# A transformer block with dilated local attention and an MLP gate: order of the layer norms, runs of the softmax sums, and the queues of two kinds of DMA

## The chip, the cores and the metric

The kernel runs on one core of one Trainium2 chip. The metric is the device time of one execution in microseconds (us). The core has a matrix engine (PE, with its weight loads shown apart as PEld), a vector engine (DVE), a scalar engine (ACT), GpSimd (POOL), and a queue processor (SP) that only issues DMAs. Every engine works through its own instructions strictly in the order in which they stand in its queue; instructions of different engines wait for each other by semaphores.

## The reference

The input is x of 2048 rows and 512 columns in bf16. What is computed, cut to what matters:

```python
def _A_ref(x, wqkv, wo):                  # 32 heads of 16, window W = 8, dilation dil = 2
    q, k, v = ...                         # x @ wqkv, split by heads
    idx = pos[:, None] - off[None, :]     # off = arange(8) * 2: rows i, i-2, ..., i-14
    logits = einsum("bhsd,bhswd->bhsw", q, kg) * Dh ** -0.5
    logits = where(mask, logits, -1e9)
    return (softmax(logits) @ vg).reshape(B, S, D) @ wo

def _B_ref(x, w1, w2, w3, w4):            # F = 1376
    h = gelu(layernorm(x) @ w1)
    hs = concat([rows -1, +1, -2, +2 of the four column groups of h]) @ w2
    x1 = x + hs
    return x1 + gelu(layernorm(x1) @ w3) @ w4

xn = layernorm(x)
out = x + _A_ref(xn) * silu(_B_ref(xn))
```

Since the dilation is 2, a row attends only to rows of its own parity. The kernel therefore splits the 2048 rows into two parities of 1024 rows (index p), in which the window is 8 neighbouring rows.

## The kernel before, in words

**Chunks.** The 1024 rows of each parity are two chunks of 512 rows, so there are four chunks c = 0 to 3 with p = c // 2. Each chunk passes through these stages:

- `stage_a(c)` (L184): the layer norm of the chunk (`layer_stats`, L173: statistics on DVE, the inverse root on POOL; the normalisation L197 on DVE), 16 transposes on PE into `tr_ps` (L203) and their copy to `xnT` (L205), a row of scales from the second layer norm (`r2`, L189 to L216), then the products for q and k (L224), and w1 with a gelu (L240, L244) into `hT`. Four stages write `hT`.
- `stage_b(c)` (L260): the product with w2 over shifted rows of `hT` (L268), the residual add on DVE (L273), a layer norm (`l3` tiles), a store of the normalised chunk to DRAM (`x1n_dram`, L281) and its transposed load as `x1nT` (L285). `stage_b(0)` needs `hT` of chunks 0 and 2; `stage_b(1)` needs chunk 3 as well.
- `stage_w3(c)` (L291): 44 products of w3 with `x1nT` (L301), each pair followed by a gelu (L306) into `h3T`.
- `w4_tile(c, jj)` (L310): one tile of 128 rows: 11 products with w4 (L317), one with the identity that adds x1 (L321), and the gate (L323 on ACT, L324 on DVE). There are 16 of them.

The tiles of the statistics of both layer norms, `st`, `mv` and `rstd`, share their tags, with two buffers each, in the pool `small`.

**Attention units.** Each parity is nine units of up to 120 query rows (the first has 128, the last 56). `scores(p, u)` (L333) makes v (L339, copied by DVE at L343), the logits `s_ps` (L359), four exponentials on ACT (L366) and two masks on DVE (L369). `weighted(p, u, ...)` (L375) makes the 32 small products `o_ps` (L387), of which each 32-row group holds 16 rows of outputs and the sums of the softmax, and copies them to two `orw` tiles, one on ACT (L396) and one on DVE (L398).

**Runs and normalisation.** The nine units of a parity form two runs: units 0 to 4 (608 rows) and units 5 to 8 (416 rows). After the last unit of a run, `normalise(p, r)` (L402) issues, all on SP's queue:

- two stores of the sums to DRAM (L410) and one load of them, spread over 128 partitions, as `dn` (L413);
- eight DMAs that repack the outputs from `orw` to `oT` (L417), 16 partitions each;
- after the reciprocal on DVE (L423), a store of it (L424) and four broadcast loads as `rr` (L427).

It ends with a DVE product of `oT` with `rr` (L431). The two `orw` tiles of a run and its `rr` take their buffers from one pool, `sm5`, with three buffers.

**The end.** `final_tile(p, i)` (L435) loads one tile of 128 rows of x as `xt` (L437, two buffers), multiplies `oT` with wo (L440, four products), multiplies with the gate (L445) and adds x (L446) on DVE into `sg` (two buffers), and stores it (L447). Load and store are on SP's queue.

**Order.** The program text gives the order of priority; at build time the framework lists the instructions of each engine in that order as its own model of the durations finds them ready and their buffers free, so an instruction can stand ahead of an earlier one that is not ready in the model. On the chip each engine keeps the list. The main body reads (L450 to L480):

```python
    for c in range(3):
        stage_a(c)
    stage_b(0); stage_a(3); stage_b(1); stage_w3(0); stage_b(2)
    stage_w3(1); stage_b(3); stage_w3(2); stage_w3(3)
    for n, (p, u) in enumerate(order):        # 18 units
        cur = (p, u) + scores(p, u)
        if fill: fill.pop(0)()                # one w4_tile for each unit
        if prev is not None: weighted(*prev)
        if n >= 13: final_tile(0, n - 13)
```

followed by the rest of the final tiles: three of the first parity and eight of the second.

## Time and profile before

| what | value |
|---|---|
| median of the two timed runs | 289.62 us (288.32 and 290.92) |
| profiled execution, its own time | 291.65 us |
| its span, first to last instruction | 289.9 us |
| mean granted clock of PE in it | 0.926 of full speed |
| busy in the span | PE 225.9, DVE 154.5, ACT 136.7, POOL 18.5 us |
| DMA moved | 21.31 MB, 73 GB/s on average |

The profile is of one execution. Its views used below are: the page with the busy time of each engine and the chain of work that ended last; a table by stage, where each row is a stretch of the span with the busy time of each engine, the granted clock (1.00 is full speed) and the busy share of the 16 DMA engines; the list of waits (who waited for whom: total us, times, longest); and the timeline. In it, PE's busy time is that of pipelined matmuls, whose single durations overlap.

### The profile page before, as it was taken

The numbers are of one execution on the slowest core, as the hardware profiler recorded it, in microseconds if no ns is written. First come the engines' busy times: TensorE is split into PE (matmuls) and PEld (weight loads), VectorE is DVE, ScalarE is ACT, GpSimd is POOL, SyncE is SP. The second block draws the span as 40 slices with busy tenths as digits, with TensorE's granted clock in tenths as the row PEclk, the third lists the DMA queues.
The fourth block names the chain that finished last, engine by engine and source line by source line (L and its number), as shares of the span: only waits on it lengthen the run. The fifth ranks groups of instructions, "written<-read, shape, count | busy, mean of one in ns | idle before, by whom it ended". The sixth has DMA issues, their size and how long they took to land.

```text
span 289.9 us, 4239 instructions
## 1 busy us (share of the span) xinstructions
PE 225.9 (78%) x1704; PEld 98.7 (34%) x1704; DVE 154.5 (53%) x273; ACT 136.7 (47%) x164; POOL 18.5 (6%) x42
## 2 busy tenths in 40 slices
PE   0599999508999899949899999889979997491470
PEld 0344444204444344414233434333334333130120
DVE  5676240666053717200276667586677777562453
ACT  1065848100836262505977777748877666200000
POOL 2344000041001010000000000000000000000000
PEclk9999999965999999989979999999999999957588
DMA  6997000025002323230000002410310126314443
GB/s 186 352 376 234 3 0 0 0 72 75 0 0 75 72 76 69 75 72 1 0 2 0 2 1 42 91 59 6 66 62 0 38 45 136 119 37 110 130 145 109
DMA packets 28387, 21.31 MB, mean 73 GB/s; under 512 B 10992, under 2 KB 27856, under 8 KB 28368
## 3 DMA queue, kind: packets, MB, share of 16 engines
q1 hardware_dynamic: 28368, 21.04, 27.2%
q8 instruction: 13, 0.21, 0.3%
q14 instruction: 6, 0.05, 0.1%
HBM read 12.39 MB, written 4.46 MB: 58 GB/s over the span
## 4 chain that ended last, share of the span: by engine, by line
PE 44%; DMA 16%; DVE 13%; SPq 11%; ACT 9%; issue 3%; POOL 2%; POOLq 0%; DVEq 0%; ACTq 0%
PE qk_ps L224 11%; PE w_ps L317 9%; PE w_ps L301 7%; SPq L417 5%; ACT prob L366 5%; PE w_ps L240 5%; DMA xt<-in_A_x_dram 4%; DMA x1nT<-x1n_dram 3%; DMA xn_85<-in_A_x_dram 3%; PE s_ps L359 3%; DVE l3s L177 3%; PE v_ps L339 2%; SPq L427 2%; PE o_ps L387 2%; DMA rr<-rden_d_2327 2%
## 5 line engine op out<-in xcount | busy, mean ns | idle before, releaser
L366 ACT ACTIVATE prob<-s_ps 128x960 bf16<-128x960 f32 (+2 forms) x72 | 61.6, 934 | 22.4 <-PE s_ps L359 19.9
L369 DVE TENSOR_TENSOR prob<-prob,mask_126 128x1920 bf16<-128x1920 bf16 (+1 forms) x32 | 34.6, 1089 | 21.6 <-ACT prob L366 21.6
L317 PE MATMUL w_ps<-w_sb,h3T 128*128 128x512 bf16 (+1 forms) x176 | 45.0, 388 | 0.4 <-DVE v_aug_131 L343 0.3
L301 PE MATMUL w_ps<-x1nT,w_sb 128*128 128x512 bf16 (+1 forms) x176 | 40.3, 391 | 5.1 <-DMA x1nT<-x1n_dram 5.1
L306 ACT ACTIVATE h3T<-w_ps 128x1024 bf16<-128x1024 f32 x20 | 20.5, 1024 | 34.8 <-PE w_ps L301 20.9
L301 PEld LDWEIGHTS <-w_sb 128*128 128x128 bf16 (+1 forms) x176 | 17.8, 102 | 27.4 <-DMA x1nT<-x1n_dram 6.3
L317 PEld LDWEIGHTS <-h3T 128*128 128x128 bf16 (+1 forms) x176 | 15.6, 99 | 21.6 <-issue 7.6
L224 PEld LDWEIGHTS <-wqk_sb 128*128 128x128 bf16 x128 | 13.7, 108 | 18.9 <-issue 6.0
L440 PE MATMUL wo_ps<-wo_sb,oT_2325 128*128 128x512 bf16 x32 | 10.3, 474 | 12.2 <-DVE sg L445 12.2
L230 ACT ACTIVATE qm_138<-qk_ps,hmask 128x1024 bf16<-128x1024 f32 x8 | 8.4, 1113 | 22.8 <-PE qk_ps L224 22.6
L224 PE MATMUL qk_ps<-xnT_133,wqk_sb 128*128 128x512 bf16 x64 | 17.0, 427 | 1.5 <-DVE xnT_133 L205 1.5
L224 PE MATMUL qk_ps<-xnT_134,wqk_sb 128*128 128x512 bf16 x64 | 16.7, 421 | 0.6 <-DVE xnT_134 L205 0.6
L230 ACT ACTIVATE qm_137<-qk_ps,hmask 128x1024 bf16<-128x1024 f32 x8 | 8.4, 1113 | 18.1 <-PE qk_ps L224 18.1
L369 DVE TENSOR_TENSOR prob<-prob,mask_123 128x2048 bf16<-128x2048 bf16 x4 | 4.9, 1224 | 21.9 <-ACT prob L366 21.9
L273 DVE TENSOR_TENSOR xn_85<-w_ps,xn_85 128x1024 bf16<-128x1024 f32 x4 | 4.9, 1215 | 21.6 <-PE w_ps L268 21.6
L440 PE MATMUL wo_ps<-wo_sb,oT_1498 128*128 128x512 bf16 x32 | 11.7, 473 | 3.7 <-DVE v_aug_131 L343 3.7
L240 PE MATMUL w_ps<-xn2T,w_sb 128*128 128x512 bf16 x64 | 14.5, 379 | 0.0
L359 PE MATMUL s_ps<-qm_137,kT_135 32*128 32x240 bf16 (+2 forms) x144 | 11.4, 266 | 3.9 <-ACT prob L366 2.5
L398 DVE CAST orw<-o_ps 128x480 bf16<-128x480 f32 (+2 forms) x18 | 11.3, 628 | 5.0 <-PE o_ps L387 4.9
L359 PE MATMUL s_ps<-qm_138,kT_136 32*128 32x240 bf16 (+2 forms) x144 | 10.1, 259 | 5.0 <-ACT prob L366 3.4
L323 ACT ACTIVATE sig<-w_ps 128x512 bf16<-128x512 f32 x16 | 9.6, 599 | 8.1 <-PE w_ps L321 8.1
L396 ACT ACTIVATE orw<-o_ps 128x480 bf16<-128x480 f32 (+2 forms) x18 | 9.5, 551 | 6.2 <-PE o_ps L387 6.2
(104 smaller groups left out, 270.1 us busy)
## 6 DMA issues: line engine op xcount, KB each, us to landing
xt<-in_A_x_dram SPq DMA_DIRECT2D x16, 128.0 KB
out_dram<-sg SPq DMA_DIRECT2D x16, 128.0 KB
w_sb<-in_B_w_dram SPq DMA_DIRECT2D x1, 1376.0 KB
w_sb<-in_B_w_dram SPq DMA_DIRECT2D x1, 1280.0 KB
xn_85<-in_A_x_dram SPq DMA_DIRECT2D x4, 256.0 KB
wqk_sb<-in_A_wqkv_dram SPq DMA_DIRECT2D x2, 512.0 KB
w_sb<-in_B_w_dram SPq DMA_DIRECT2D x2, 512.0 KB
xn_86<-in_A_x_dram SPq DMA_DIRECT2D x4, 256.0 KB
```

The costliest lines, as they stand in the source:

```text
L224: nc.tensor.matmul(pt[:, b, :], lhsT=wqk_sb[:, dt, nt * P : (nt + 1) * P], rhs=xnT[p][:, dt, cs], start=(dt == 0), stop=(dt == ND - 1),)
L230: nc.scalar.activation(qm[p][:, 2 * a : 2 * a + 2, e, cs], pt, AF.Copy, scale=hmask[:, e : e + 1])
L240: nc.tensor.matmul(pt[:, b, :], lhsT=w1_sb[:, dt, g * P : (g + 1) * P], rhs=xn2T[:, dt, :], start=(dt == 0), stop=(dt == ND - 1),)
L301: nc.tensor.matmul(pt[:fs, ft % 2, :], lhsT=w3_sb[:, dt, ft * P : ft * P + fs], rhs=x1nT[:, dt, :], start=(dt == 0), stop=(dt == ND - 1),)
L306: last["gelu"] = nc.scalar.activation(h3T[:, 2 * a : 2 * a + 2, :], pt, AF.Gelu_apprx_tanh)
L317: nc.tensor.matmul(pt, lhsT=h3T[:fs, ft, jj * P : (jj + 1) * P], rhs=w4_sb[:fs, ft, :], start=(ft == 0), stop=False,)
L359: nc.tensor.matmul(st[:nk, b, dl * 2 * nq : (dl + 1) * 2 * nq].rearrange("k (e q) -> k e q", e=2), lhsT=kT[p][r : r + 32, dt, k0 : k0 + nk ...
L366: nc.scalar.activation(prv[:nk, jj], st[:nk, :, 0 : 4 * nq], AF.Exp, scale=SCALE)
L369: nc.vector.tensor_tensor(out=ph[:nk], in0=ph[:nk], in1=msk[:nk, 0:nq].unsqueeze(1).to_broadcast([nk, 16, nq]), op=ALU.mult,)
L398: nc.vector.tensor_copy(out=dst, in_=src)
L417: nc.sync.dma_start(out=oT[p][DH * hh : DH * (hh + 1), :, ra : ra + rw], in_=orw[p][jj][32 * cg : 32 * cg + DH, :, 0:rw],)
L440: nc.tensor.matmul(pt, lhsT=oT[p][:, dt, i * P : (i + 1) * P], rhs=wo_sb[:, dt, :], start=(dt == 0), stop=(dt == ND - 1),)
```

## The change

1. **Layer norms.** The statistics and the normalisation of `stage_a` move to a new function `stage_ln(c)`; the tiles of `l1` and `l3` get tags of their own. `stage_ln(3)` is emitted ahead of `stage_a(2)`.
2. **Order of w2 and w3.** `stage_b(2)` is emitted before `stage_w3(0)`, and `stage_b(3)` before `stage_w3(1)`.
3. **Runs.** The second parity gets three runs: units 0 to 4 (608 rows), 5 and 6 (240 rows), 7 and 8 (176 rows). The product with `rr` becomes `normalise_end`, emitted later: for the run (0, 0) at unit index 9, for (0, 1) at 13, for (1, 0) at 17, and for (1, 1) and (1, 2) among the last final tiles.
4. **Queues.** The repack DMAs (L417) are issued by POOL instead of SP. The loads of x for the end become two DMAs of 1 MB (`load_xo`, SP's queue), and the stores become eight DMAs of two tiles each on ACT's queue.
5. **Fill.** Of the w4 tiles 13 are filled in at unit indices 0 to 12 and three come after the last unit; all final tiles come after that.
6. **Buffers.** The pool `sm5` (`orw`, `rr`) goes from three buffers to four, `sm4` (weights w1 and w2, `xn2T`, `xn3`, `x1nT`, `prob`) from six to five.

```diff
-    for a, b in ((0, (NU + 1) // 2), ((NU + 1) // 2, NU)):
-        runs.append((a, b, units[a][0], sum(units[u][1] for u in range(a, b))))
-    RW = max(r[3] for r in runs)
+    for cuts in ((0, 5, NU), (0, 5, 7, NU)):
+        runs.append(
+            [(a, b, units[a][0], sum(units[u][1] for u in range(a, b))) for a, b in zip(cuts[:-1], cuts[1:])]
+        )
+    RW = max(r[3] for rs in runs for r in rs)
...
-    sm5 = ctx.enter_context(tc.tile_pool(name="sm5", bufs=3))
-    sm4 = ctx.enter_context(tc.tile_pool(name="sm4", bufs=6))
+    sm5 = ctx.enter_context(tc.tile_pool(name="sm5", bufs=4))
+    sm4 = ctx.enter_context(tc.tile_pool(name="sm4", bufs=5))
...
-        st = small.tile([P, TPC, nc.vector.BN_STATS_DIM], F32, name=name + "s", tag="st")
-        mv = small.tile([P, TPC, nc.vector.BN_AGGR_DIM], F32, name=name + "m", tag="mv")
+        st = small.tile([P, TPC, nc.vector.BN_STATS_DIM], F32, name=name + "s", tag=name + "s")
+        mv = small.tile([P, TPC, nc.vector.BN_AGGR_DIM], F32, name=name + "m", tag=name + "m")
...
-    def stage_a(c):
+    r2s = {}
+
+    def stage_ln(c):
         p, k = c // 2, c % 2
         x_c = xn[p][:, k * TPC : (k + 1) * TPC, :]
...
         rsqrt_eps(r2, r2)
+        for j in range(TPC):
+            nc.vector.tensor_scalar(
+                out=x_c[:, j, :], in0=x_c[:, j, :], scalar1=mv[:, j, 0:1], scalar2=rstd[:, j : j + 1],
+                op0=ALU.subtract, op1=ALU.mult,
+            )
+        r2s[c] = r2
...
-                nc.sync.dma_start(
+                nc.gpsimd.dma_start(
                     out=oT[p][DH * hh : DH * (hh + 1), :, ra : ra + rw],
                     in_=orw[p][jj][32 * cg : 32 * cg + DH, :, 0:rw],
                 )
...
+    def normalise_end(p, r):
+        _, _, ra, rw = runs[p][r]
         nc.vector.tensor_tensor(
-            out=oT[p][:, :, ra : ra + rw], in0=oT[p][:, :, ra : ra + rw], in1=rr[:, :, 0:rw], op=ALU.mult
+            out=oT[p][:, :, ra : ra + rw], in0=oT[p][:, :, ra : ra + rw], in1=rrs[p, r][:, :, 0:rw], op=ALU.mult
         )
 
+    def load_xo(p):
+        xo[p] = midt([P, M // P, D], f"xo{p}")
+        nc.sync.dma_start(out=xo[p], in_=xv[p].rearrange("(i q) d -> q i d", q=P))
+
     def final_tile(p, i):
-        xt = fin.tile([P, D], BF16, name="xt", tag="xt")
-        nc.sync.dma_start(out=xt, in_=xv[p, i * P : (i + 1) * P, :])
...
-        nc.vector.tensor_tensor(out=sg, in0=sg, in1=xt, op=ALU.add)
-        nc.sync.dma_start(out=ov[p, i * P : (i + 1) * P, :], in_=sg)
-
-    for c in range(3):
-        stage_a(c)
+        nc.vector.tensor_tensor(out=xo[p][:, i, :], in0=sg, in1=xo[p][:, i, :], op=ALU.add)
+        if i % 2 == 1:
+            nc.scalar.dma_start(
+                out=ov[p, (i - 1) * P : (i + 1) * P, :].rearrange("(i q) d -> q i d", q=P),
+                in_=xo[p][:, i - 1 : i + 1, :],
+            )
+
+    stage_ln(0)
+    stage_a(0)
+    stage_ln(1)
+    stage_ln(2)
+    stage_a(1)
+    stage_ln(3)
+    stage_a(2)
     stage_b(0)
     stage_a(3)
     stage_b(1)
+    stage_b(2)
     stage_w3(0)
-    stage_b(2)
+    stage_b(3)
     stage_w3(1)
-    stage_b(3)
     stage_w3(2)
     stage_w3(3)
...
+    fill = {n: [w4s[n]] for n in range(13)}
+    fill[5].append(lambda: load_xo(0))
+    fill[9].append(lambda: load_xo(1))
+    fill[9].append(lambda: normalise_end(0, 0))
+    fill[13] = [lambda: normalise_end(0, 1)]
+    fill[17] = [lambda: normalise_end(1, 0)]
...
-        if n >= 13:
-            final_tile(0, n - 13)
     weighted(*prev)
-    for f in fill:
+    for f in w4s[13:]:
         f()
-    for i in range(len(order) - 13, M // P):
+    for i in range(M // P):
         final_tile(0, i)
-    for i in range(M // P):
+    normalise_end(1, 1)
+    for i in range(6):
+        final_tile(1, i)
+    normalise_end(1, 2)
+    for i in range(6, M // P):
         final_tile(1, i)
```

More of the change, by code (lines that the diff above doesn't have):

```diff
@@ L192, in stage_a @@
         rsqrt_eps(r2, r2)
+        for j in range(TPC):
[4 more added lines that the diff above has]
+        r2s[c] = r2
+    def stage_a(c):
+        p, k = c // 2, c % 2
+        x_c = xn[p][:, k * TPC : (k + 1) * TPC, :]
+        cs = slice(k * CH, (k + 1) * CH)
+        r2 = r2s.pop(c)
         for h in range(TPC // 2):
@@ L376, in weighted @@
         q0, nq, k0, nk = units[u]
-        r = 0 if u < runs[0][1] else 1
-        ra = runs[r][2]
-        if u == runs[r][0]:
+        r = next(i for i, x in enumerate(runs[p]) if u < x[1])
+        ra = runs[p][r][2]
+        if u == runs[p][r][0]:
             orw[p] = [sm5.tile([P, ND, RW], BF16, name="orw", tag="s5") for jj in range(2)]
@@ L398, in weighted @@
                 nc.vector.tensor_copy(out=dst, in_=src)
-        if u == runs[r][1] - 1:
+        if u == runs[p][r][1] - 1:
             normalise(p, r)
+    rrs = {}
     def normalise(p, r):
-        _, _, ra, rw = runs[r]
+        _, _, ra, rw = runs[p][r]
         if r == 0:
@@ L466 @@
         cur = (p, u) + scores(p, u)
-        if fill:
-            fill.pop(0)()
+        for f in fill.get(n, ()):
+            f()
         if prev is not None:
```

13 lines of the change are left out of this document (5 added, 8 removed).

## The prediction

> **What bounds the kernel now.** I read the page first: the busy shares, then the chain that ended last.
>
> ```profile
> PE 225.9 (78%) x1704; PEld 98.7 (34%) x1704; DVE 154.5 (53%) x273; ACT 136.7 (47%) x164; POOL 18.5 (6%) x42
> PE 44%; DMA 16%; DVE 13%; SPq 11%; ACT 9%; issue 3%; POOL 2%; POOLq 0%; DVEq 0%; ACTq 0%
> ```
>
> PE is busiest, yet holds only 44% of the chain; DMA and SP's queue hold 27%. So I cut the span into stages and looked for stretches in which PE rests.
>
> ```profile
> 26.20:38.68 12.48, 11.81 (x69) 5.86 (x68) 4.21 (x10) 8.13 (x8) 1.03 (x1) 1.00 0.06 21
> 54.77:65.16 10.39, 0.01 (x2) 0.01 (x1) 8.02 (x23) 0.00 (x0) 2.88 (x6) 0.73 0.15 50
> 65.16:81.17 16.01, 15.07 (x69) 7.31 (x70) 4.77 (x11) 7.21 (x7) 1.32 (x3) 0.75 0.27 34
> 81.17:84.62 3.45, 3.45 (x17) 1.57 (x16) 1.49 (x2) 1.03 (x1) 0.00 (x0) 1.00 0.00 0
> 84.62:94.12 9.50, 9.50 (x46) 4.38 (x45) 5.07 (x13) 4.77 (x5) 1.27 (x2) 1.00 0.17 57
> 121.00:123.35 2.35, 2.32 (x11) 0.88 (x9) 0.69 (x1) 0.84 (x2) 0.00 (x0) 1.00 0.04 13
> 123.35:127.57 4.22, 0.00 (x1) 0.01 (x1) 0.00 (x0) 0.00 (x0) 0.00 (x0) 1.00 0.65 124
> 127.57:138.86 11.29, 11.29 (x45) 4.75 (x46) 0.00 (x0) 4.86 (x5) 0.00 (x0) 0.85 0.00 1
> 145.00:220.30 75.30, 68.25 (x768) 28.55 (x765) 53.18 (x65) 54.14 (x73) 0.00 (x0) 0.98 0.15 32
> 220.30:257.40 37.10, 28.82 (x341) 12.40 (x341) 25.39 (x36) 20.77 (x29) 0.00 (x0) 0.95 0.29 67
> 257.40:289.90 32.50, 13.68 (x40) 4.67 (x40) 13.55 (x26) 0.00 (x0) 0.00 (x0) 0.71 0.42 118
> ```
>
> Columns: stretch, length, busy PE, PEld, DVE, ACT, POOL, granted clock, DMA share, GB/s. The first row is an undisturbed `stage_a` (chunk 1): 12.48 us. PE then rests 10.39 us before that of chunk 3, which takes 16.01 us at a clock of 0.75. It rests 4.22 us before the last `stage_w3`, which takes 11.29 us where the first took 9.50. From 257.40 on PE is busy 13.68 of 32.50 us. The waits name the causes:
>
> ```profile
> PE tr_ps L203 <- DVE xn_86 L197: 10.4, 1, 10.4
> PE w_ps L301 <- DMA x1nT<-x1n_dram: 5.1, 2, 4.2
> PE wo_ps L440 <- DVE sg L445: 12.2, 3, 6.2
> DVE sg L445 <- DMA out_dram<-sg: 9.6, 5, 4.0
> PE wo_ps L440 <- DVE v_aug_131 L343: 3.7, 1, 3.7
> 53.09 1.24 DVE xn_85 L273
> 58.16 0.58 DVE l1s L177
> 63.62 1.05 POOL l1r L171
> ```
>
> The last three rows are of the chain: DVE does chunk 3's statistics only at 58, behind `stage_b(0)`'s add at 53.09, although x was there long before; the shared tags with two buffers explain it.
>
> **The change part by part: the front.** LN(3) is emitted ahead of `stage_a(2)`, with own tags. Its DVE and POOL work lands where DVE is busy 4.21 of 12.48 us; that PE-bound stage hides it. Chunk 3 then starts at 54.77 and is done 12.48 us later instead of 10.39 + 16.01 = 26.40: 13.9 gone. What is late next is DVE, which still owes `stage_b(0)` its work when the transposes are done:
>
> ```profile
> L273 DVE TENSOR_TENSOR xn_85<-w_ps,xn_85 128x1024 bf16<-128x1024 f32 x4 | 4.9, 1215 | 21.6 <-PE w_ps L268 21.6
> L177 DVE BATCH_NORM_STATS2 l3s<-xn_85 128x6 f32<-128x512 bf16 x8 | 5.2, 672 | 0.1
> 26.85 1.30 DVE xnT_133 L205 x2
> 111.23 0.69 DVE l3s L177
> 123.10 4.42 DMA x1nT<-x1n_dram
> ```
>
> One add (1.2) and three statistics (2.0) hold the copies `xnT` back, which otherwise start 0.65 behind the transposes (26.85 after 26.20): 2.5 us lost (0 to 4). Gain 11.4.
>
> `stage_b(2)` and `stage_b(3)` each move one `stage_w3` forward. From the last statistics' start at 111.23 to the landing of `x1nT` (123.10 + 4.42) are 16.3 us, now covered by two `stage_w3` of 9.50. So b1, b2, w3, b3, three w3 take 3 x 3.45 + 4 x 9.5 = 48.4 us, plus 0.5 for PSUM buffers that wait on two adds in a row, against 138.86 - 81.17 = 57.7: 8.8 gone. The 2.35 us of attention work that PE did while waiting must be done again, of which the ramp of the first unit hides half: 1.1. Front in all: 11.4 + 8.8 - 1.1 = **19.1** (16 to 21). Five `sm4` buffers hold w2, three `x1nT` and one `xn3` here, and four `prob` tiles later: nothing.
>
> **The loop, units 1 to 12** (145.00 to 220.30). One w4 tile a unit, as before; 6.1 us a unit, between these starts:
>
> ```profile
> 170.19 3.56 ACT L366 ACTIVATE prob<-s_ps 128x960 bf16<-128x960 f32 x4 [1.12 <-PE s_ps L359]
> 171.59 2.27 PE w_ps L317 x10
> 176.28 3.56 ACT L366 ACTIVATE prob<-s_ps 128x960 bf16<-128x960 f32 x4 [1.12 <-PE s_ps L359]
> L366 ACT ACTIVATE prob<-s_ps 128x960 bf16<-128x960 f32 x56 | 50.0, 978 | 17.4 <-PE s_ps L359 16.2 <-PE o_ps L387 1.2
> L396 ACT ACTIVATE orw<-o_ps 128x480 bf16<-128x480 f32 x14 | 7.8, 573 | 0.2 <-PE o_ps L387 0.2
> ```
>
> Twelve units at 6.1 make 73.2 less 1 for the short one, so about 3 us are lost around the runs' ends, where the next run's `orw` waits for its buffer and DVE for `rr`. The later `normalise_end` and the fourth buffer give back part: **1.8** (0 to 3.5). The two loads of x (1 MB each) run where DMA is 15% busy: nothing.
>
> **POOL's DMAs.** No row shows a DMA issued there. The nearest:
>
> ```profile
> L417 SPq DMA_DIRECT2D oT_2325<-orw x16: 586/598/1867, 234.1 to 263.8; - x16
> L171 POOL TENSOR_TENSOR l1r<-l1r,nhalf 128x4 f32<-128x4 f32 x4 | 4.2, 1039 | 0.2
> 200.14 1.64 SPq L410 DMA_DIRECT2D den_d_1864<-orw  x2
> 211.50 3.25 DMA rr<-rden_d_1865
> 233.49 1.92 DMA den_d_2326<-orw
> ```
>
> Lower end 0.59 us (SP's usual issue), upper 1.87 (SP's longest); I take 1.04, POOL's own costliest instruction. Of a run's two `orw` tiles one finds a free buffer, the other waits for four repacks of the run before and their landing (2 us, as the store of the sums at 233.49): 4 x 1.04 + 2 = 6.2, against a unit of 6.1 twice and of some 4.6 twice (below). That is 3.2 us, held in the sums here; at 1.87 it is 16.5; at 0.59 it is nothing. What waits is DVE's copy L398, and behind it in DVE's order the masks and v of the next unit.
>
> The Trainium skill's "SBUF — State Buffer", in "A bandwidth-pool intuition that's wrong", has a POOL-issued DMA of 620 ns taking about 3100 ns beside a DVE copy, and its "Who interferes with whom" limits that to DVE operations in a two-port mode, a two-input product not among them. By 3.1 us the waits would cost 36 us and eat the gain; by the second section my 1.04 stands, as DVE's loop is products and reads of PSUM. No run here shows it yet.
>
> **The end, from 220.30 on** (69.6 us before). Units 13 to 17 lose their w4 and final tiles; ACT is next: 3.56 for four exponentials + 0.57 = 4.1, with half of the gap of 1.12 some 4.6. Four units, 2.5 for the short one (56 of 120 columns), 2 for the last `weighted`, 2 of buffer waits: 25. (The product of run (1, 0) stands at 18 and its `rr` comes at 5 + 14.6, the length of a run's chain below; that wait is in the 2 as well.) Then three w4 tiles at 12 x 0.227 = 2.7 and eight final tiles:
>
> ```profile
> L445 DVE TENSOR_TENSOR sg<-wo_ps,xn_86 128x512 bf16<-128x512 f32 x8 | 5.3, 687 | 4.5 <-DMA out_dram<-sg 4.4
> L446 DVE TENSOR_TENSOR sg<-sg,xt 128x512 bf16<-128x512 bf16 x16 | 6.5, 416 | 1.2 <-DMA xt<-in_A_x_dram 0.9
> L431 DVE TENSOR_TENSOR oT_2325<-oT_2325,rr 128x1664 bf16<-128x1664 bf16 x1 | 1.0, 1026 | 3.6 <-DMA rr<-rden_d_2654 3.6
> 286.79 0.42 DVE sg L446
> ```
>
> A final tile costs DVE 0.69 + 0.42 = 1.1 once no buffer of `sg` or `xt` stands in SP's queue. 8.2 + 8.8 = 17.0, less 2 that PE takes ahead inside the units: done at 40. Eight more: 8.8, and products of 1.0 in all (by width from 1.03 for 1664): 49.8. From the last add's end (287.21) to 289.90 are 2.7 us; a store of twice the size gets 3: 52.8. The gain is 69.6 - 52.8 = **16.8** (10 to 22). Three runs instead of two add eight POOL and eight SP issues and a reciprocal beside PE's work. A store on ACT waits for DVE's add; behind it in ACT's order stand only other stores.
>
> Does the last run's chain hide? From 200.14 to 214.75 (211.50 + 3.25) a run took 14.6 us with the repacks in SP's queue; from 25 that is 39.6, and its product is wanted at 47. Cover 7 us; without it, each us shows.
>
> The Trainium skill's "DMA: Bandwidth & Descriptors", "Issuing engines are not separate DMA queues", says that another issuing engine saves only issue time. That speaks against gain from moved stores if the 16 engines were the limit; the row from 257.40 has them at 0.42, so it agrees that issue and buffers, not bandwidth, are what goes.
>
> **Sum.** 19.1 + 1.8 + 16.8 = 37.7. The profiled execution took 291.65 (span 289.9 and 1.75 around it), so 253.9; it lies 2.0 above the median, 289.62, from which I count: **252 us**.
>
> **The rivals.**
> - *POOL is slow, 1.87 us a DMA*: 16.5 - 3.2 = 13.3 more: 265. For it: L417's longest row. Against: POOL does nothing else there.
> - *The front stays*: LN(3) is still listed behind `stage_b(0)`, so 11.4 are missing: 263. The planner decides; against it, the tags no longer tie them.
> - *Slower*: the same wait at 3.5 us a DMA. At price c the loss is 2(4c - 4.1) + 2(4c - 2.6) - 3.2, and what the last run's repacks, 8c + 2, take beyond the 22 us from 25 to 47: 39.4 + 8.0 = 47.4, so 252 + 47 = 299. It decides from c = 3.1 (no change) and 3.35 (2% slower). Against: nearly twice the longest issue in L417's row. (The Trainium skill's 3100 ns, named above from "SBUF — State Buffer", would be the point of no change, if its rule held for this loop.)
>
> **How the numbers follow.** Forecast 0.72; slow POOL 0.13; front stays 0.09; slower 0.03; something between that leaves it within 2% 0.03. The bounds of the terms added give gains of 26 to 46.5: 243 to 264; the two middle rivals lie at 263 and 265, so 243 to 266. Leaving out the slower cases and the tails of the forecast, that holds 0.8. Two per cent (5.8 us) is about what a measurement of this kernel tells from no change. Faster 0.94, same 0.03, slower 0.03.
>
> **What would show it.** No wait of `tr_ps` on L197 near 55 us; none of L301 on `x1nT`; the first `s_ps` near 118; units 13 to 16 starting 4.6 apart; final tiles 1.1 apart on DVE; no DVE wait on `rr` over 2 us. Wrong it would be by DVE idle before L398 released by a repack, POOL rows longer than 2 us, or final tiles waiting for a store.

## The result, and the profile after

| | before | after |
|---|---|---|
| median of the timed runs | 289.62 us (288.32 and 290.92) | 258.72 us (257.70 and 259.73) |
| profiled execution | 291.65 us | 259.73 us |
| its span | 289.9 us | 258.0 us |
| mean granted clock of PE | 0.926 | 0.958 |

The ratio after to before is 0.8933, with a 95% interval of 0.8704 to 0.9161. The forecast was 252 us in a range of 243 to 266: the sign and the range held, and the time is 6.7 us above the value. Of these 6.7, 5.8 lie between the profiled executions (253.9 forecast, 259.73); the rest is that the sum went to the median by the 2.0 us that the profiled execution before lay above its own, and this one lies 1.0 above. Behind this small miss stand a front and an end that came to the sizes forecast, and a loop that lost where a gain was forecast.

The page of the kernel after, busy times and the chain that ended last:

```profile
PE 222.5 (86%) x1704; PEld 98.3 (38%) x1704; DVE 152.8 (59%) x275; ACT 136.0 (53%) x164; POOL 39.9 (15%) x82
PE 56%; DVE 15%; ACT 10%; DMA 9%; issue 4%; POOL 3%; SPq 2%; DVEq 0%; ACTq 0%
```

PE's work is the same to 3.4 us, but it now holds 56% of the chain instead of 44%; DMA and SP's queue fell from 27% to 11%. The table by stage (stretch, length, busy PE, PEld, DVE, ACT, POOL, granted clock, DMA share, GB/s) shows where:

```profile
54.40:71.35 16.95, 13.43 (x69) 6.23 (x66) 8.20 (x19) 7.09 (x7) 1.26 (x2) 0.90 0.24 62
91.21:118.90 27.69, 27.69 (x130) 12.77 (x129) 4.90 (x13) 15.31 (x17) 1.26 (x2) 1.00 0.24 58
161.90:187.48 25.58, 20.04 (x210) 7.83 (x211) 14.45 (x19) 12.71 (x19) 0.71 (x2) 0.87 0.20 68
180.00:185.00 5.00, 5.00 (x15) 1.62 (x15) 2.45 (x2) 2.67 (x3) 0.00 (x0) 0.50 0.00 0
205.68:235.00 29.32, 25.66 (x284) 10.96 (x284) 19.77 (x25) 19.86 (x28) 8.73 (x18) 0.83 0.26 58
```

**Front.** Chunk 3's products start at 54.40, so the wait of 10.39 us ahead of them is gone; they take 16.95 us, not the undisturbed 12.48. The last three `stage_w3` run in 27.69 us with PE busy throughout: the wait for the last `x1nT` is gone. Unit 1's first exponential moves from 145.03 to 125.80: 19.2 us.

**Loop.** Units 7 to 9 stretch over the third row: 25.58 us. The same units took 19.30 before:

```profile
181.82:201.12 19.30, 16.90 (x208) 7.32 (x208) 13.66 (x18) 12.79 (x19) 0.00 (x0) 1.00 0.23 54
```

In all, from unit 1 to unit 13, 75.3 us became 79.9 (125.80 to 205.68): 4.6 lost, where 1.8 were to be gained.

**End.** From unit 13's first exponential to the end of the span, 69.6 us became 52.3 (205.68 to 258.0): 17.3 gained. Units 13 to 17 with the last w4 tiles, the last row of the table, ran at a clock of 0.83.

19.2 - 4.6 + 17.3 = 31.9, the difference of the two spans (289.9 and 258.0). So the question is units 7 to 9. The timeline of the kernel after there (start, length, engine, line, what; in brackets the idle time ahead of it and what ended it):

```profile
165.60 0.39 SPq L455 DMA_DIRECT2D xo_1830<-in_A_x_dram  x1
166.04 2.54 SPq L439 DMA_DIRECT2D rr<-rden_d_1502  x4
...
167.19 1.02 PE L349 MATMUL v_ps<-wv_sb,xnT_133 128*64 128x512 bf16 x4 [1.41 <-DVE xn_85 L334]
168.49 1.83 ACT L376 ACTIVATE prob<-s_ps 128x960 bf16<-128x960 f32 x2 [1.61 <-PE o_ps L397]
...
174.34 1.43 DVE L447 TENSOR_TENSOR oT_1500<-oT_1500,rr 128x2432 bf16<-128x2432 bf16 x1 [2.83 <-DMA rr<-rden_d_1502]
175.68 0.65 DVE L408 CAST orw<-o_ps 128x480 bf16<-128x480 f32 x1
176.25 0.67 DVE L353 CAST v_aug_129<-v_ps 64x512 bf16<-64x512 f32 x1
176.98 0.81 PE L349 MATMUL v_ps<-wv_sb,xnT_134 128*128 128x512 bf16 x3 [2.54 <-DVE v_aug_129 L353]
180.83 4.45 PE L327 MATMUL w_ps<-w_sb,h3T 128*128 128x512 bf16 x10
```

Read downwards: the second load of x (1 MB, `xo_1830`) leaves SP at 165.60, directly ahead of the four loads of `rr` of run (0, 0). DVE reaches that run's product (L447) and stands 2.83 us, because `rr` isn't there. Behind the product in DVE's order stand the copies of `orw` and of v; PE waits 2.54 us for that v. After this thin stretch the clock is 0.50 in 180 to 185, and ten w4 products take 4.45 us, where they took 2.27. A row of the waits and one of the chain show how SP came to issue the load there, and what it cost:

```profile
SPq L455 <- PE w_ps L331: 1.9, 1, 1.9
168.00 6.12 DMA rr<-rden_d_1502
```

The load itself waited 1.9 us on SP for its buffer, with the loads of `rr` behind it; the last of these then took 6.12 us to land, beside 1 MB of x. The first load of x shows no such harm: from unit 1 to unit 7 are 36.1 us (125.80 to 161.90), 36.8 before.

### The profile page after: what moved, and what is told of

The parts are those of the page before. It is cut to its first block, busy times and chain, and to the rows that moved or that the text cites. A ratio compares the mean times of both kernels' runs of the same rounds, so it can differ in the third digit from the quotient of the medians.

```text
span 258.0 us, 4290 instructions
## 1 busy us (share of the span) xinstructions
PE 222.5 (86%) x1704; PEld 98.3 (38%) x1704; DVE 152.8 (59%) x275; ACT 136.0 (53%) x164; POOL 39.9 (15%) x82
## 4 chain that ended last, share of the span: by engine, by line
PE 56%; DVE 15%; ACT 10%; DMA 9%; issue 4%; POOL 3%; SPq 2%; DVEq 0%; ACTq 0%
PE w_ps L311 14%; PE w_ps L327 13%; PE qk_ps L234 9%; ACT prob L376 7%; PE w_ps L278 5%; PE w_ps L250 4%; PE s_ps L369 4%; DVE l1s L179 3%; DMA rr<-rden_d_1502 2%; PE o_ps L397 2%; PE v_ps L349 2%; DVE orw L408 2%; SPq L439 1%; DMA oT_2286<-orw 1%; ACT orw L406 1%
## 5 line engine op out<-in xcount | busy, mean ns | idle before, releaser
L376 ACT ACTIVATE prob<-s_ps 128x960 bf16<-128x960 f32 (+2 forms) x72 | 61.8, 951 | 18.2 <-PE s_ps L369 15.2
L327 PE MATMUL w_ps<-w_sb,h3T 128*128 128x512 bf16 (+1 forms) x176 | 49.1, 412 | 0.2
L311 PE MATMUL w_ps<-x1nT,w_sb 128*128 128x512 bf16 (+1 forms) x176 | 38.3, 379 | 0.0
L316 ACT ACTIVATE h3T<-w_ps 128x1024 bf16<-128x1024 f32 x20 | 20.5, 1023 | 25.6 <-PE w_ps L311 23.3
L311 PEld LDWEIGHTS <-w_sb 128*128 128x128 bf16 (+1 forms) x176 | 17.6, 100 | 20.4
L327 PEld LDWEIGHTS <-h3T 128*128 128x128 bf16 (+1 forms) x176 | 16.1, 102 | 22.6 <-issue 9.4
L429 POOL DMA_DIRECT2D oT_1500<-orw x16 | 8.3, 526 | 86.3 <-ACT orw L406 86.3
L353 DVE CAST v_aug_129<-v_ps 128x512 bf16<-128x512 f32 (+1 forms) x9 | 6.1, 681 | 23.0 <-PE v_ps L349 23.0
L234 PE MATMUL qk_ps<-xnT_133,wqk_sb 128*128 128x512 bf16 x64 | 17.0, 428 | 1.1 <-DVE xnT_133 L215 1.1
L429 POOL DMA_DIRECT2D oT_2286<-orw x24 | 12.1, 512 | 36.9 <-ACT orw L406 35.2
L234 PE MATMUL qk_ps<-xnT_134,wqk_sb 128*128 128x512 bf16 x64 | 16.1, 409 | 0.7 <-DVE xnT_134 L215 0.7
L369 PE MATMUL s_ps<-qm_138,kT_136 32*128 32x240 bf16 (+2 forms) x144 | 12.6, 278 | 3.5 <-ACT prob L376 1.7
L408 DVE CAST orw<-o_ps 128x480 bf16<-128x480 f32 (+2 forms) x18 | 11.2, 625 | 3.6 <-PE o_ps L397 3.0
L349 PE MATMUL v_ps<-wv_sb,xnT_134 128*128 128x512 bf16 (+1 forms) x36 | 11.1, 385 | 2.5 <-DVE v_aug_129 L353 2.5
L369 PE MATMUL s_ps<-qm_137,kT_135 32*128 32x240 bf16 (+2 forms) x144 | 10.2, 260 | 3.0 <-DVE orw L408 1.6
```

What stands on the lines that cost most here:

```text
L234: nc.tensor.matmul(pt[:, b, :], lhsT=wqk_sb[:, dt, nt * P : (nt + 1) * P], rhs=xnT[p][:, dt, cs], start=(dt == 0), stop=(dt == ND - 1),)
L311: nc.tensor.matmul(pt[:fs, ft % 2, :], lhsT=w3_sb[:, dt, ft * P : ft * P + fs], rhs=x1nT[:, dt, :], start=(dt == 0), stop=(dt == ND - 1),)
L316: last["gelu"] = nc.scalar.activation(h3T[:, 2 * a : 2 * a + 2, :], pt, AF.Gelu_apprx_tanh)
L327: nc.tensor.matmul(pt, lhsT=h3T[:fs, ft, jj * P : (jj + 1) * P], rhs=w4_sb[:fs, ft, :], start=(ft == 0), stop=False,)
L349: nc.tensor.matmul(vp[:nk, :], lhsT=xnT[p][:, dt, k0 : k0 + nk], rhs=wv_sb[:, dt, :], start=(dt == 0), stop=(dt == ND - 1),)
L369: nc.tensor.matmul(st[:nk, b, dl * 2 * nq : (dl + 1) * 2 * nq].rearrange("k (e q) -> k e q", e=2), lhsT=kT[p][r : r + 32, dt, k0 : k0 + nk ...
```

## The experiments

The theory from the traces: the load of x, placed in the middle of run (0, 0)'s chain, is what the loop lost. The rivals: VectorE's new order costs it whatever the load does; or the queue of GpSimd does. Further runs take the parts of the gain apart. Each run is timed beside runs of the kernel before on the same chip; all differences below are of medians unless they are marked as parts of one profiled span.

**1. The second load of x into a buffer of another pool.**

```diff
-        xo[p] = midt([P, M // P, D], f"xo{p}")
+        xo[p] = (midt if p == 0 else bigt)([P, M // P, D], f"xo{p}")
```

> The changed kernel with one edit: the second load of x takes its buffer from the pool of xnT and kT, which falls free only after unit 8, instead of from a pool that has a free buffer at unit 8. Theory: this 1 MB load stands on SP's queue directly ahead of the four loads of rr of run (0, 0); it delays them by some 3 us, DVE waits in order for them, PE runs dry and its clock falls, and units 7 to 9 take 25.6 us instead of 19.3. Then rr lands within about 3.3 us of its last issue, the granted clock from unit 9 to 10 is back at 1.00, and the time is 252.5 us (251 to 254). Rival 1: it is the place at which the product with rr stands in DVE's order; then the wait stays and the time is 257 to 259. Rival 2: it is the orw buffers; then nothing changes, 258.7 us.

Measured: 253.55 us (252.59 to 254.70), ratio 0.8815 (0.8739 to 0.8891); loop 75.6 us. The size came as the theory said, a detail did not: the load left the queue behind the loads of `rr` (SP's rows), but the last load of `rr` on the chain still took 6.14 us to land, and DVE still waited.

```profile
164.26 2.55 SPq L439 DMA_DIRECT2D rr<-rden_d  x4
167.85 0.39 SPq L455 DMA_DIRECT2D xo<-in_A_x_dram  x1
166.23 6.14 DMA rr<-rden_d
172.69 1.43 DVE L447 TENSOR_TENSOR oT<-oT,rr 128x2432 bf16<-128x2432 bf16 x1 [1.61 <-DMA rr<-rden_d]
161.06:182.38 21.32, 17.59 (x206) 7.43 (x211) 14.34 (x19) 12.63 (x19) 0.71 (x2) 0.92 0.27 82
```

So there are two harms: standing ahead in the queue, and sharing the DMA engines. The first is the smaller: the loads of `rr` left SP 2.52 us behind the store of the reciprocals in the kernel after (163.52 to 166.04) and 1.58 here (162.68 to 164.26), 0.9 less. The next run removes both.

**2. The second load of x behind run (0, 1)'s last load of `rr`.**

```diff
-            nc.sync.dma_start(                      # rr
+            last["rr"] = nc.sync.dma_start(
...
-        nc.sync.dma_start(out=xo[p], in_=xv[p].rearrange("(i q) d -> q i d", q=P))
+        src = xv[p].rearrange("(i q) d -> q i d", q=P)
+        if p == 0:
+            nc.sync.dma_start(out=xo[p], in_=src)
+        else:
+            with tc.issue_after(last["rr"].ins):
+                nc.sync.dma_start(out=xo[p], in_=src)
...
-    fill[9].append(lambda: load_xo(1))
+    fill[11].append(lambda: load_xo(1))
```

> One edit to the changed kernel: the second load of x (1 MB) keeps SyncE's queue, but is issued only behind the last reciprocal load of run (0,1), so it neither holds that run's own loads in the queue nor shares the DMA engines with the run (0,0)'s, and its buffer is free by then. Theory (the load of x in the middle of run (0,0)'s two hops is what the loop lost): units 7 to 10 come back to 19.3 to 20.5 us (25.6 in the changed kernel, 21.3 with the load in another buffer but still beside the reciprocals), the reciprocals of run (0,0) land in under 4.5 us (6.1), the granted clock in these units stays over 0.95, and the time is 250.5 to 253.5 us. Rival (the place of run (0,0)'s product in VectorE's order costs it, whatever the load does): units 7 to 10 stay over 23 us and the time over 255.5 us. Second rival (the load, now later, meets the reciprocals of run (1,0) or the first final tiles): the loop is mended, but the end from unit 13 grows from 52.3 to over 55 us, and the time is 255 to 258 us.

Measured: 253.74 us (252.88 to 254.06), ratio 0.8805 (0.8762 to 0.8848), span 251.9. SP's rows, DVE's product and the stretch of units 7 to 9:

```profile
165.83 2.55 SPq L439 DMA_DIRECT2D rr<-rden_d  x4
191.72 0.46 SPq L460 DMA_DIRECT2D xo<-in_A_x_dram  x1
170.68 0.67 DVE L353 CAST v_aug<-v_ps 64x512 bf16<-64x512 f32 x1
172.67 1.41 DVE L447 TENSOR_TENSOR oT<-oT,rr 128x2432 bf16<-128x2432 bf16 x1
162.73:181.45 18.72, 15.99 (x204) 7.04 (x208) 14.00 (x19) 12.64 (x20) 0.72 (x2) 1.00 0.12 37
126.62:199.64 73.02, 64.80 (x753) 28.22 (x765) 53.68 (x66) 53.83 (x74) 8.33 (x16) 1.00 0.20 47
```

The product has no bracket any more: DVE doesn't wait, so `rr` had landed at most 4.3 us behind the end of its last issue (168.38 to 172.67); counted the same way it took 5.5 in the kernel after (168.58 to 174.12) and 5.6 in run 1. Units 7 to 9 take 18.72 us at full clock, less than the 19.3 that the theory named. The whole loop takes 73.0 us, 2.3 less than before the change. The median is 0.2 us above the theory's band, as the front of this run came 0.8 us later (unit 1 at 126.62). The end stayed at 52.3, so the second rival is out.

One caution: with the load, the lists of PE and DVE changed as well. In the kernel after, PE's products for v (L349) stand ahead of those of `o_ps` (L397) in unit 7, and the third exponential of that unit starts 6.59 us after the first (161.90 and 168.49); in runs 1 and 2 the order is the other way round and it starts 4.41 us after (161.06 and 165.47; 162.73 and 167.14). So of the 6.9 us between the kernel after (25.6) and run 2 (18.7), 2.2 belong to the order that the planner (the framework that lists the instructions) chose when the load was elsewhere. The other 4.7 lie behind that point, with the waits for `rr` and the clock in them: 2.1 between the kernel after and run 1, 2.6 between runs 1 and 2.

DVE's product moved too. In the kernel after it stands ahead of the copy of v for unit 8 (174.34 and 176.25), in runs 1 and 2 behind it (170.68 and 172.67 above), so the place of the product, the first rival, isn't ruled out by the time alone. The traces show what each part does. In the kernel after the last `rr` landed 10.6 us behind the store of the reciprocals (163.52 to 174.12), in run 2 at most 8.4 (164.24 to 172.67). With 8.4 it would have been there by 171.95, and DVE, free from 171.51 on, would have waited some 0.4 us in place of 2.83 (an estimate from these rows). So most of the wait is the load's doing; that PE felt it, through v, is the place's. How the 4.7 us divide between the two is open: no run keeps both lists and moves the load alone.

**3. The repacks back on SP.**

```diff
-                nc.gpsimd.dma_start(
+                nc.sync.dma_start(
                     out=oT[p][DH * hh : DH * (hh + 1), :, ra : ra + rw],
```

> The changed kernel with the repack DMAs back on SP's queue, all else as it is. Theory: eight issues of 0.6 us stand again between the load of the sums and the store of the reciprocals; each run's rr lands 3 to 5 us later. The last run has no cover left (DVE waited 0.5 us for its rr), so 4 us more there, and 2 to 4 more around unit 8: 265 us (262 to 268). Rival: the chain of a run hides everywhere but at unit 8, and the queue is worth nothing: 259 us.

Measured: 276.77 us (275.78 to 277.49), ratio 0.9618 (0.9541 to 0.9696): 18 us slower than the kernel after, far outside what was expected. The loop is as long as in the kernel after (125.39 to 204.75, 79.4 us), though laid out otherwise (units 7 to 9 take 22.6 us, units 10 to 12 20.6 where 18.2), so taking the repacks off GpSimd doesn't bring the loop's loss back; the end takes 69.4 us, as long as before the change. SP's rows and DVE's products of the second parity:

```profile
216.38 5.73 SPq L429 DMA_DIRECT2D oT<-orw  x7
227.05 0.56 SPq L422 DMA_DIRECT2D den_d<-orw  x1
233.01 0.54 SPq L422 DMA_DIRECT2D den_d<-orw  x1
243.50 7.57 SPq L439 DMA_DIRECT2D rr<-rden_d  x4
251.17 2.18 SPq L422 DMA_DIRECT2D den_d<-orw  x2
...
230.99 1.43 DVE L447 TENSOR_TENSOR oT<-oT,rr 128x2432 bf16<-128x2432 bf16 x1 [8.14 <-DMA den_d<-orw]
265.42 0.53 DVE L447 TENSOR_TENSOR oT<-oT,rr 128x704 bf16<-128x704 bf16 x1 [5.19 <-DMA rr<-rden_d]
```

The product of run (1, 0) waits 8.14 us (the row names the store that landed last; what the product reads is `rr`, whose loads had left SP by 226.95), and PE waits 7.17 us for a mask behind it. The last run's sums leave SP at 251.17; in the kernel after they left at 237.05. With three runs in one queue, each run's sums, repacks and reciprocals stand behind those of the run before. But the 18 us are not the queue's waiting alone: the planner listed PE otherwise, with 31 of the final products ahead of the last `o_ps` (251.12) where one stands in the kernel after (235.40), and two stores stand ahead of the last copies on ACT, which wait 5.66 us. How much each is worth isn't separated.

**4. The front alone**: the kernel before with the layer norms and the stage order, no other edit (the diff is parts 1 and 2 of the change).

> The kernel before with the layer norm edits and the order of w2 and w3 alone; runs, queues, buffers and the end as before. Theory: the front's gain is independent of the rest; the first exponential of unit 1 comes 19 us earlier and the rest keeps its length: 270 us (268 to 272). Rival: part of it is given back later, since the loop then runs closer to the loads or waits longer for its buffers: 274 us or more.

Measured: 271.43 us (270.94 to 271.88), ratio 0.9434 (0.9364 to 0.9505), span 270.0: 19.9 us less than before in the span, 17.6 on medians. Unit 1 at 125.36, end 69.8 us.

**5. The layer norms alone**: as run 4, but with the old order of `stage_b` and `stage_w3`.

```diff
     stage_b(1)
-    stage_b(2)
     stage_w3(0)
-    stage_b(3)
+    stage_b(2)
     stage_w3(1)
+    stage_b(3)
     stage_w3(2)
```

> The kernel before with the layer norms emitted first and in tiles of their own, but the old order of the second and third stages (w3 of chunk 0 ahead of the second stage of chunk 2, and so on). It splits the front's gain (17.6 us on medians, 19.9 in the profiled spans) into its two edits. By the prediction's terms the layer norms give 11.4 and the stage order 8.8 less 1.1 for work done there at present: 277 to 280 us. Rival (chunk 3's 16.95 us of products in the changed kernel, 4.5 over the undisturbed 12.48, show that the layer norms gave only 9.4; the order then gave the rest): 279.5 to 281.5 us. Second rival (the two overlap: with the layer norms early, the wait for the last normalised chunk is there in full or grows): under 276 or over 282 us.

Measured: 279.13 us (276.90 to 280.42), ratio 0.9657 (0.9575 to 0.9740). Unit 1's first exponential stands at 133.58: 11.45 us earlier than before, and 8.2 later than in run 4. The theory's terms, 11.4 and 7.7, held. The wait of PE for the normalised chunk is still there in this run, 3.9 us against 5.1 before:

```profile
PE w_ps L309 <- DMA x1nT<-x1n_dram: 3.9, 2, 3.3
```

**6. The repacks on GpSimd, with the old end**: run 4 and one edit, the same line as in run 3 the other way.

```diff
-                nc.sync.dma_start(
+                nc.gpsimd.dma_start(
                     out=oT[p][DH * hh : DH * (hh + 1), :, ra : ra + rw],
```

> The kernel before with the new layer norms and stage order (front_only, 271.4 us) and one edit: the repacks are issued by GpSimd. The end is the old one: runs of nine and eight units, products at once behind the reciprocals, five final tiles inside the loop, x and stores by SyncE tile by tile. Theory (what the end gained is a joint effect: with the repacks on SyncE the new end loses 18 us, and with the old end the repacks alone are only 4.8 us of SyncE beside the final tiles' own loads and stores): 266 to 270 us, since each run's chain gets shorter by at most the 16 issues that stand between its sums and its reciprocals (some 3 to 4 us in the last run, of which the wait for the load of x and for the store buffers takes part back). Rival (the queue move is the whole of it, and the rest of the new end, which made no difference where two of its parts were undone, is worth nothing): 254 to 260 us. Third (GpSimd's repacks come later than SyncE's, or share the engines with the reciprocals): 271 us or more.

Measured: 265.78 us (265.30 to 267.27), ratio 0.9212 (0.9146 to 0.9278): 0.2 us below the theory's band and far from both rivals. With runs 3 and 4 and the kernel after this makes a table of four, all with the new front (medians; for the kernel after the mean, 259.0, of its two medians, 258.72 and 259.30 in run 12):

| | repacks on SP | repacks on POOL |
|---|---|---|
| old end | 271.4 | 265.8 |
| new end | 276.8 | 259.0 |

The queue move is worth 5.6 us with the old end and 17.8 with the new one; the new end costs 5.4 without it and gains 6.8 with it. Neither has a price of its own.

**7. The products at once, not deferred.**

```diff
+        normalise_end(p, r)                         # at the end of normalise
...
-    fill[9].append(lambda: normalise_end(0, 0))
-    fill[13] = [lambda: normalise_end(0, 1)]
-    fill[17] = [lambda: normalise_end(1, 0)]
...
-    normalise_end(1, 1)
-    for i in range(6):
-        final_tile(1, i)
-    normalise_end(1, 2)
-    for i in range(6, M // P):
+    for i in range(M // P):
         final_tile(1, i)
```

> One edit to the changed kernel: the products with the reciprocals are emitted at once behind the reciprocals' loads, as in the kernel before, in place of two to four units later and between the final tiles. Theory (the place only matters where the reciprocal isn't there yet when VectorE comes to it; the order is planned again around it, and the load of x delays the first run's reciprocals in any case, so that VectorE stands 2 to 4 us at each of the second parity's first two runs while units 14 to 17 queue behind it): 261 to 266 us, with the loss between units 13 and 17. Rival (the planner moves the products to the same places by its own costs): 258 to 259.5 us. Second rival (an earlier product lets the first parity's final tiles start earlier): 254 to 257.5 us.

Measured: 264.37 us (263.69 to 265.16), ratio 0.9146 (0.9073 to 0.9220): 5.4 slower, in the theory's band, and of its span 4.4 us are lost from unit 13 on (206.72 to 263.4, 56.7 us).

```profile
231.52 1.43 DVE L448 TENSOR_TENSOR oT<-oT,rr 128x2432 bf16<-128x2432 bf16 x1 [5.13 <-DMA oT<-orw]
233.52 0.23 PE L397 MATMUL o_ps<-prob,v_aug 64*32 64x56 bf16 x8 [2.75 <-DVE prob L379]
255.30 0.52 DVE L448 TENSOR_TENSOR oT<-oT,rr 128x704 bf16<-128x704 bf16 x1 [0.23 <-DMA rr<-rden_d]
```

DVE stands 5.13 us at the product of run (1, 0), 3.61 in the kernel after, and the last product comes at 255.30 instead of 249.89. The place of the loss is not the theory's: the last unit's first exponential follows unit 13's by 16.8 us in both kernels. What stands behind the product here is the last mask, for which PE waits 2.75 us; the eleven w4 products behind that take 4.24 us, where eleven took 2.54 in the kernel after. The wait and the 1.7 us of slower products make the 4.4.

**8. The stores back on SP.**

```diff
-            nc.scalar.dma_start(
+            nc.sync.dma_start(
                 out=ov[p, (i - 1) * P : (i + 1) * P, :].rearrange("(i q) d -> q i d", q=P),
```

> One edit to the changed kernel: the eight final stores are issued by SyncE again, in place of ScalarE. Theory (a store that waits for its final tile stands in SyncE's queue ahead of the last run's denominators and reciprocals, whose chain has no cover left in the changed kernel: its product waited 0.5 us for them): the last run's denominators leave SyncE 3 to 6 us later, VectorE waits as much before the last product, and the time is 261 to 264.5 us. Rival (the emission order leaves the stores of the first parity done before the last run's denominators are ready, so that they block nothing): 258 to 259.5 us, no change. Second rival (ScalarE gains from being rid of the 8 issues): 256 to 257.5 us.

Measured: 258.16 us (256.45 to 259.35), ratio 0.8959 (0.8898 to 0.9020): no difference, as the first rival said; my theory fell. SP's rows show why:

```profile
237.66 1.12 SPq L422 DMA_DIRECT2D den_d<-orw  x2
238.89 0.39 SPq L468 DMA_DIRECT2D out_dram<-xo  x1
240.21 0.33 SPq L425 DMA_DIRECT2D dn<-den_d  x1
242.41 0.39 SPq L468 DMA_DIRECT2D out_dram<-xo  x1
243.09 0.32 SPq L436 DMA_DIRECT2D rden_d<-rb  x1
245.30 2.54 SPq L439 DMA_DIRECT2D rr<-rden_d  x4
```

The last run's sums left ahead of the first store, and each later store falls into a pause in which SP waits for the chain anyway.

**9. Two runs in the second parity** instead of three.

```diff
-    for cuts in ((0, 5, NU), (0, 5, 7, NU)):
+    for cuts in ((0, 5, NU), (0, 5, NU)):
...
-    normalise_end(1, 1)
-    for i in range(6):
+    for i in range(4):
         final_tile(1, i)
-    normalise_end(1, 2)
-    for i in range(6, M // P):
+    normalise_end(1, 1)
+    for i in range(4, M // P):
         final_tile(1, i)
```

> One edit to the changed kernel: the second parity is normalised in two runs (units 9 to 13, then 14 to 16 with 17) instead of three, four final tiles standing between the two products. Theory (the third run exists so that the first of the two late chains of denominators starts two units early; with one run its whole repack, of more heads, starts only after the last unit, and the chain that had 0.5 us of slack is later by some 2 us for the extra repacks on GpSimd's queue): the last product waits 2 to 4 us more and the time is 260 to 262.5 us. Rival (a run less saves its own product, its reciprocal and its hops, some 1.5 to 2.5 us of VectorE and SyncE, and the final tiles cover the longer chain): 256 to 257.5 us. No difference: 258 to 259.5 us.

Measured: 259.32 us (258.39 to 260.12), ratio 0.8993 (0.8941 to 0.9045): no difference, the third outcome named; both the theory and its rival fell. The one late product waits 0.59 us for its `rr`:

```profile
244.78 1.03 DVE L447 TENSOR_TENSOR oT<-oT,rr 128x1664 bf16<-128x1664 bf16 x1 [0.59 <-DMA rr<-rden_d]
```

**10. The second stage's layer norm apart**: `stage_b`'s statistics, normalisation, store and reload become `stage_bn(c)`, emitted behind `stage_b(c)`, for chunk 0 behind `stage_a(3)`.

```diff
-        mv, rstd = layer_stats(x_c, "l3")
+    def stage_bn(c):
+        p, k = c // 2, c % 2
+        x_c = xn[p][:, k * TPC : (k + 1) * TPC, :]
+        mv, rstd = layer_stats(x_c, "l3")
...
     stage_b(0)
     stage_a(3)
+    stage_bn(0)
     stage_b(1)
+    stage_bn(1)
     stage_b(2)
+    stage_bn(2)
```

> The changed kernel with the layer norm of stage_b (statistics, normalisation, store and transposed load) as a function of its own, emitted after stage_a(3) for chunk 0 and directly behind the w2 products for the others. Theory: after the move of LN(3) DVE's debt to stage_b(0) is what is late, 16.95 us for the products of chunk 3 against 12.48; with the statistics behind the copies 3 to 4 us of it go: 255.5 us (254.5 to 257). Rival: DVE pays the debt later, and the first w3 products wait for PSUM buffers: 258.7 us.

Measured: 257.16 us (256.18 to 258.13), ratio 0.8944 (0.8853 to 0.9035). Chunk 3's products take 13.29 us instead of 16.95, and unit 1 stands 3.55 earlier, at 122.25. Part of this is lost again in units 7 to 9, which here take 26.4 at a clock of 0.81:

```profile
54.35:67.64 13.29, 11.76 (x68) 5.86 (x68) 8.36 (x19) 7.10 (x7) 1.27 (x2) 1.00 0.11 39
158.35:184.75 26.40, 21.27 (x206) 8.35 (x211) 14.45 (x19) 12.71 (x19) 0.71 (x2) 0.81 0.20 66
```

On medians the gain of 1.9 (259.0 to 257.16) isn't told from nothing; the stage that it aimed at shows it plainly.

**11. Runs 2 and 10 together.**

> The edit of x_after together with that of bn_late (the layer norm of each chunk's second stage taken out of it, chunk 0's behind the first stage of chunk 3). If the two gains are independent (bn_late took 3.5 us off the time up to the first exponential; the load of x costs 5 to 6 us in units 7 to 10), unit 1's first exponential stands at 122 to 123 us, units 7 to 10 take 19.3 to 20.5 us, and the time is 247.5 to 250.5 us. Rival (the slot that one frees is lost again in the end, whose length is set by the chain of the last run and not by when the loop ends): 251 to 254 us, with the stretch from unit 13 at 54 us or more.

Measured: 249.35 us (248.99 to 249.72), ratio 0.8658 (0.8618 to 0.8697). This beats both kernels, the kernel after by 9.7 us (259.0 to 249.35). In the spans the two gains add up: unit 1 stands 3.4 us earlier, at 122.37, units 7 to 9 take 6.9 less, as in run 2, and the end takes the same 52.3 us (195.38 to 247.70). That is 10.3, the difference of the spans (258.0 and 247.7):

```profile
158.48:177.19 18.71, 16.00 (x204) 7.04 (x208) 13.99 (x18) 12.63 (x19) 0.71 (x2) 1.00 0.11 37
```

**12. The kernel after once more**, unedited.

> The changed kernel once more, unedited, beside the same runs of the kernel before: the base that the runs with single edits are held against, whose median so far rests on two executions (257.70 and 259.73 us). Expected 257 to 260 us. If it is under 257 us, the gain of the later layer norm of the second stage (1.6 us on medians) isn't told from nothing; over 260, the runs with the stores on SyncE and with two sums in the second parity would count as gains.

Measured: 259.30 us (258.58 to 260.17), ratio 0.8980 (0.8918 to 0.9042): inside what was expected. Against this interval, runs 1, 2 and 11 are faster than the kernel after, runs 3 and 7 slower, and runs 8, 9 and 10 not told from it.

## Why the prediction was right, and where it was not

**The front, 19.1: right in its sum (19.2), in part by luck.** Run 5 gives 11.45 for the layer norms (11.4 forecast) and, against run 4, 8.2 for the order (8.8 - 1.1 = 7.7 forecast). By stages of the kernel after, the terms lie otherwise. Chunk 3's products end 9.8 us earlier (81.17 and 71.35), not 11.4, for DVE's debt to `stage_b(0)` held them up by 4.5 us (16.95 - 12.48), where "2.5 us lost (0 to 4)" was set. The stages of w2 and w3 take 10.1 us less (57.7 before, 71.35 to 118.90 after), not 8.8, and the step from there to unit 1 takes 0.7 more (6.2 and 6.9), not 1.1. That makes 19.2: a first term 1.6 too high, made up by the other two. In run 5, too, 1.2 of the 11.45 are a shorter wait for `x1nT` (5.1 and 3.9), which the first term hadn't. The mechanism of the debt was the one named, for when the layer norm behind `stage_b(0)` comes later (run 10), chunk 3 falls to 13.29.

**The loop, +1.8: wrong (-4.6), and nearly the whole miss.** The step that failed reads: "The two loads of x (1 MB each) run where DMA is 15% busy: nothing." The mean share of the DMA engines was no measure. The second load stood in SP's queue directly ahead of the four loads on which DVE's product depends, and then shared the engines with them. Without that meeting (run 2) the loop takes 73.0 us against 75.3 before, a gain of 2.3 where 1.8 was forecast, and 1.8 less than the 74.8 of run 4, which has the new front and the old loop: the rest of the term was sound in size. 2.2 of the 6.9 us in question go with another order of PE's products, and the product's other place on DVE has a share in the rest (see run 2).

**The price of a DMA on POOL, 1.04 us: too high, and harmless.** The rows of the kernel after for the forty repacks (line, engine, what; shortest, median, longest ns; first and last start):

```profile
L429 POOL DMA_DIRECT2D oT_2286<-orw x24: 512/512/514, 213.9 to 239.3; - x24
L429 POOL DMA_DIRECT2D oT_1500<-orw x16: 512/512/727, 155.6 to 190.3; - x16
...
DMA to landing us min/median/max: 1.7/2.8/4.0
```

At 0.51 us, under my lower end of 0.59, the waits of `orw` for its buffer (3.2 us in my sum) should vanish, and the list of waits has none of DVE's copies L408 on a repack. The slow-POOL rival and the slower one are out with these rows. So is, as a time for which a DMA holds POOL, the 3100 ns of the Trainium skill's "SBUF — State Buffer", "A bandwidth-pool intuition that's wrong", for this loop: the longest of forty is 727 ns.

**The end, 16.8: right in its sum (17.3), with errors that cancel.** The marks of the sum held: from unit 13 on, the first eight final tiles are done at 40.9 us (40 forecast), the last add at 49.0 (49.8), the store at 52.3 (52.8). What lies under them did not all hold, and that they meet is in part luck. Units 13 to 15 start 3.86 us apart (205.68, 209.54, 213.39), not 4.6. Against that, the clock, which the sum took as full, was 0.83 up to 235, and DVE stood 3.61 us at the product of run (1, 0), where 2 us were set for all buffer waits:

```profile
DVE oT_2286 L447 <- DMA oT_2286<-orw: 3.6, 1, 3.6
DVE oT_2286 L447 <- DMA rr<-rden_d_2579: 0.5, 1, 0.5
L465 DVE TENSOR_TENSOR sg<-wo_ps,xn_86 128x512 bf16<-128x512 f32 x8 | 5.3, 685 | 0.2
L466 DVE TENSOR_TENSOR xo_1830<-sg,xo_1830 128x512 bf16<-128x512 bf16 x8 | 3.1, 417 | 0.0
```

The final tiles cost 0.685 + 0.417 = 1.10 us each with next to no idle time between, as worked out. (The first row names a repack as what landed last; in run 9, where the row names `rr`, DVE stands 3.19 us at this product, against the sign "no DVE wait on `rr` over 2 us".) The last run's chain had no cover of 7 us: its product waited 0.5 for `rr`. The chain itself was shorter than the 14.6 forecast (from 237.05 to 249.89, 12.8), but it started 31.4 us behind unit 13 and not 25, as PE did two of the last w4 tiles (229.91 to 235) ahead of the last unit's `o_ps`.

**What the sum hid.** "The end" was one term with one list of edits, each with a price. Runs 3, 4 and 6 show that the prices don't add: with the repacks on SP's queue the new end is a loss of 5.4 us. Two of its edits, the stores on ACT and the third run, are worth nothing that these runs can tell; the later product is worth 5.4.

The Trainium skill's "DMA: Bandwidth & Descriptors", "Issuing engines are not separate DMA queues", which the prediction weighed, is borne out by the stores (run 8: nothing). It says that another issuing engine only saves issue time; for the repacks (17.8 us in the new end) the forty issues saved SP 24 us by the row of run 3, whose median is 596 ns, against 20 on GpSimd (forty at 512 ns). What the move changed besides is that the sums and reciprocals no longer stand in line with them, and the lists that the planner made; how the 17.8 divide isn't shown.

```profile
L429 SPq DMA_DIRECT2D oT<-orw x40: 585/596/1837, 156.7 to 258.7; - x40
```

## What to carry to other kernels

A transfer is not free because the DMA engines are idle on average: look up which load with a waiting reader stands next to it in its queue, and give it a place behind that load by an explicit dependence. In a queue that works in order, price a set of edits together where they feed the same chain: deferring products, cutting runs and moving stores cost 5 us here while the repacks stood in SP's queue, and gained 7 once they had left it. When a load moves, look at every engine's list again: here the planner moved products on two engines with it. A wait in such a loop can cost more than itself, since the matrix engine's clock may fall behind it: 2.8 us of waiting stood in a stretch that lost 4.7.

## What the runs showed of the hardware that was not expected

- GpSimd issues a DMA of 16 partitions in 0.51 us, faster than SP (0.60), and its landing took 1.7 to 4.0 us (median 2.8). DVE's products and its reads of PSUM beside it didn't slow it: DVE was busy 37.8 of the 52.3 us of the end, and the 24 issues there took 512 to 514 ns.
- The loads of `rr` land 5.6 us behind the end of their last issue when 1 MB of x is under way, although they were issued ahead of it (run 1); without it, in at most 4.3 (run 2).
- The clock fell to half without a long pause. From 174 to 179 PE was busy 2.35 of 5 us, with 2.54 us as the longest single wait; in the stretch 180 to 185, shown above, the clock was 0.50, although PE was then busy throughout:

```profile
174.00:179.00 5.00, 2.35 (x45) 1.06 (x45) 4.66 (x7) 1.16 (x3) 0.00 (x0) 0.95 0.00 0
```

In run 2, without the wait, it stayed at 1.00 over the same units. The end has a second such place: from 222 to 226 the clock was 0.50 with PE busy throughout, after PE had been busy 1.81 of the 4 us before, with 0.88 us as the longest single wait. The Trainium skill's "TensorE: Matmul & The Clock Gate", in its Part 1 on the clock gate, has the clock go to half after an idle window of about 3.4 us. No pause of that length stands in these rows; here the clock fell after thin stretches.
